# Keys of the second batch by TensorE, x1 of the last batch by VectorE, and a new order of steps

## The chip, the cores and the metric

The kernel runs on one core of a Trainium2 chip. The metric is the device time of one execution in microseconds (us). Its engines are TensorE (PE: matrix products), VectorE (DVE), ScalarE (ACT), GpSimd (POOL) and SyncE (SP, whose queue issues nearly all DMAs here, one after the other). On-chip memory is SBUF; products land in PSUM.

## The reference

Three blocks follow one another on 4 batches of 768 tokens with 384 channels, all in fp32:

```python
# 1. linear attention, 8 heads of 48 channels
state = alpha[:, :, t, :, None] * state + einsum('bhd,bhe->bhde', k_t, v_t)
y[:, :, t] = einsum('bhd,bhde->bhe', q_t, state)          # for t in 0..767
# 2. low-rank token mix (rank 32), then an MLP 384 -> 1536 -> 384
u = x + ((x.T @ U) @ V).T
x1 = u + maximum(u @ w_ch1, 0) @ w_ch2
# 3. phases and a complex token mix, then a channel product
theta = x1 @ w_theta
y = w_tok_r @ (x1 * cos(theta)) + w_tok_i @ (x1 * sin(theta))
u = x1 + y
out = u + maximum(u @ w_ch, 0)
```

## The kernel before, in words

**Layout.** Channels lie on the partitions. Each batch has three tiles of 128 channels, and so three stored head pairs (p0 to p2, two heads of 64 and 48 rows each); the rows that are left of three pairs make a fourth pair, p3, whose keys `kp` and queries `qp` are put together by small copies of 16 rows between tiles (line 241; its decays `tp`, line 306). Its result `xp` goes back into the three tiles `X` by six such copies (line 461).

**Attention.** Time is cut into 6 chunks of 128. Lines 227 and 230 load `al`, `kk`, `qq` and `vv`. Scans and products turn keys and queries into a form without the decay (`G`, line 265; `kk`, 267; `al`, 275; `qq`, 276). Per pair: scores A (line 326) and a mask into `Am` (332 to 336), keys turned by 128 x 128 (into `kt`), increments D (377), their scan into `S` (384 on ScalarE, 387 on VectorE), and Y (397 within a chunk, 405 from the state), copied into `X` or `xp` (407).

**Two ways to turn a tile.** TensorE multiplies it with the identity into PSUM and ScalarE copies it out (keys: 358 to 365; x1: 840). Or VectorE transposes blocks of 32 x 32 (`turn`, line 250), four small DMAs put them in place in DRAM (`place`, 257), and a load brings the turned tile back (keys: 344, then a copy of the spare part by ScalarE, 351; x1: 823). Batch 0's keys go the first way and those of batches 1 to 3 the second; x1 of batches 0 to 2 goes the second way and that of batch 3 the first.

**The rest.** `xt` (544) and `g` (551) are the rank-32 products and 527, 528 the lift that adds them. The MLP runs in halves of 384 tokens over 12 blocks: `h` and `acc`, each product as three in a 1-pass format with high and low parts (668 to 670). x1 is spilled to DRAM. Theta `th`, its sine and cosine (854 to 865), and the complex token mix as seven products `mx` (978), each with its own factor sums; some of these sums are made by accumulating DMAs on GpSimd's queue (908). Last the channel product `ch` and the result (1020).

**What sets the order.** Every part is a Python generator that issues some instructions at each step. `ORDER` is a string with one letter per step: D loads, P prepares, A and B are two pairs of attention in turn, R spare copies, U and L weights, 0, 1, 2 and K the rank products, M and N the two MLP halves, H theta, V and S factors and sums, G the seven products, Y and C the outputs. Where a generator needs something, it draws another one itself. Each engine and the SyncE queue take their instructions in the order in which the steps issue them. Tables such as `BY_Q` say for each operation whether VectorE (V) or GpSimd (P) does it; in `BY_A`, A stands for ScalarE and GpSimd. A DMA waits on one of eight semaphores in turn, so for the DMA eight before it.

Of the kernel before, what the change touches and what calls it, by code (L numbers as in the profile page):

```python
# [36 lines left out]


ORDER = """
DRAPRBURAARPPBARQDAAPBBBURBRARUBUPRAAPQUAUALABBUBBBAAQQAAABLBDABLPLLAPA01BDP01AL2200R11QL2LAL201AALPABR2B210BB  # L40
MLLLRRALLAMNLDLLAAMMQLRBPMMLBMMLBRLPNMMNQLLLLNLMNLLLNMMLLMLMNLMNLMMLMLMLMMTARAAAMPRMNBABBBBDTPBNANBATABQARWBNA
WBWPNNPKNKNABBNNNQNKNKBNKKKKKDBAKRRDAPRPRBAKNBBBBAAKAKAKAQBANMBMPBPMMAMMRBMDQAKMAMBRAPABAMRBWPAMMBMABRKWBKAQBW
MANMABFABBNKABXKAKAMKFFBTTNFMBTTMMKKBNKWNNKNMMNNKKKNKMTKNKMMMNWTWTKNNMKNMNKNMMNHMNNMMTNKKNNNNMMTTTHMKTTMMHKMKM
MMHKMKMNMMTNTNMKNKKTNNNKHMNNMKNNNHKNKNNNHNNKNHNKKNNNHTHNTMTNNMNHNHNMNXHHMMTHMTTTMHTNTMTNNTHNTMTTMHHTMNMHHMMHNM
VVNNNTHTHHMTTMHHXMTHMTTMNNVNNHNVMHXTNHHHVMVVMHMHNHGNVVHGHTGVGHGGHHTGGGHHVGGVHTHGGVVHHGGGSVVVHGHGGHSVGSVVGVVGVH
HGGHGVVHSHGHVXVGGXVGVGSSGGGVVGGGGGGGGVGGVVGVGVVVGGGSGVYVGSGVGGGSVGGSVVVVXGGGGGVVGGGGGVVGGVGVGGGVSVGGGGGGVVGGVS
VGVGVVGGVVVGGGGGGVGGGGGVYGVGGVTVVVVVGGTGGGGVGVVVYGTVVGGYVVGYVGGGGGVGGGTCCGYYVCGCCGYCCCYCCGCGGGGGGYCCCCCYCYCCCC
CCCC
"""
# [7 lines left out]
BY_X = "PPPPVVVPVVVVPPPVVVVPVVVV"
BY_T = "PVPVPVVVVPVPPVVPVVVVPVVVVVVVVVVVVPVVVVVVVP"
BY_U = "VVVVVPPVVPPV"
BY_S = "VVPVPPVPVPVVVPPPVPVPPPVV"  # L60
# [9 lines left out]
def linear_attention_moe_kernel(ctx, tc, aT, kT, qT, aF, kF, qF, vP, vT, U, V4, w1, w2, wth, wtr, wti, wch, out):  # L70
# [208 lines left out]
    def prep_k(b, i):  # L279
        pr[b, i] = ld.pop((b, i)) + (T("G"),)  # L280
        if b + i:
            scale_k(b, i, 0, S)
        else:
            pool.memset(pr[b, i][3][:, HT - 1:HT], 1.0)
            for x, y in halves(b, i):
                scale_k(b, i, x, y)
                scale_q(b, i, x, y)
        KK[b, i] = pr[b, i][1]
        if b:
            t, keysT[b, i] = turn(KK[b, i][:, 0:(NC - 1) * C], f"kt{b}_{i}", 128)  # L290
# [26 lines left out]
    def att_pe(b, p):  # L317
# [105 lines left out]
        yield
        ms.append(scores(1))
# [273 lines left out]
    def contract(pend=pend):  # L698
        b, hf, f, h = pend.pop(0)
        if f == 0:  # L700
            acc[b, hf] = [PS("acc") for _ in range(KD)]
        for j in range(KD):
            w = [x[:, j * 128:(j + 1) * 128] for x in W2[f]]
            three(acc[b, hf][j][:, 0:HT], w, (h[:, 0], h[:, 1]), f == 0, f == NF - 1)
        done_with(h)
        used(W2, f)
        if f == NF - 1:
            for j, t in enumerate(acc.pop((b, hf))):
                x = X[b][j][:, hf * HT:(hf + 1) * HT]
# [106 lines left out]
    def theta(b):  # L816
        for hf in range(2):
            xs = []
            turned_x = b in range(B - 1)
            for s in range(hf * 3, hf * 3 + 3) if turned_x else ():  # L820
                if b % 2 == 0:
                    ZR[b // 2, s] = two(T("zr"))
                sync.dma_start(ZR[b // 2, s][:, b % 2], turned[f"x1t{b}_{hf}"][(s - hf * 3) * C:(s - hf * 3 + 1) * C])
            for j in range(KD):
                t = two(T("x1s", F32R))
                split(X[b][j][:, hf * HT:(hf + 1) * HT], t[:, 0], t[:, 1],
                      e_lo=dve if b in range(B) and BY_X[(b * 2 + hf) * KD + j] == "V" else pool)
                xs.append(t)
            yield 600
            for q in range(3):  # L830
                s = hf * 3 + q
                th = PS("th")
                for j in range(KD):
                    w = TH[j]
                    l = xs[j][:, :, q * C:(q + 1) * C]
                    three(th[:, 0:DM], (l[:, 0], l[:, 1]), (w[:, 0], w[:, 1]), j == 0, j == KD - 1)
                if not turned_x:
                    xt = PS("x1t")
                    for j in range(KD):
# [24 lines left out]
                for t, x in ((zi, zi), (zr, co)):  # L864
                    dve.tensor_tensor(out=t, in0=x, in1=xc, op=ALU.mult)
                done_with(n)
                if not turned_x:
                    done_with(xt)
                if b in range(B):
                    made.add((b, s))  # L870
                    if b == B - 1:
                        plus(ZR[1, s], ZI[1, s])
                else:
                    zh, zl = two(T("zh", F32R)), two(T("zl", F32R))
                    split(z, zh, zl, e_hi=act)
# [130 lines left out]
    def outputs():  # L1006
        for k, hf in ((0, 0), (1, 1), (1, 0), (0, 1)):
            while len(CH) < KD:
                next(gens["T"], None)
            while (k, hf, KD - 1) not in UQ:  # L1010
                next(gens["Y"], None)
            us = [UQ.pop((k, hf, j)) for j in range(KD)]
            for q in range(2):
                for e in range(KD):
                    t = PS("ch")
                    for j in range(KD):
                        w = CH[j][:, :, e * 128:(e + 1) * 128]
                        three(t[:, 0:HT], (w[:, 0], w[:, 1]), (us[j][0][:, q], us[j][1][:, q]), j == 0, j == KD - 1)
                    ot = T("ot")[:, 0:HT]
                    dve.scalar_tensor_tensor(out=ot, in0=t[:, 0:HT], scalar=0.0, in1=XQ[k, hf][e][:, q],  # L1020
                                             op0=ALU.max, op1=ALU.add)
                    done_with(t)
                    sync.dma_start(out[2 * k + q, e][:, hf * HT:(hf + 1) * HT], ot)
                    done_with(ot)
                    yield
# [379 lines left out]
```

## Time and profile before

| | |
|---|---|
| median of 3 runs | 667.82 us (667.09 to 669.35) |
| profiled execution | 665.01 us |
| its span | 662.9 us |
| TensorE busy | 630.8 us, 95% of the span |
| VectorE, ScalarE, GpSimd busy | 438.0, 267.2, 156.1 us |
| TensorE's mean granted clock | 0.987 |

The profile is of one execution; 2.1 us of it lie outside the span. TensorE is the busiest engine by far, so what counts is the time in which it waits, and the stretches in which its granted clock is below 1. Busy time of the other engines counts only where TensorE waits for them.

### The profile page before, as it was taken

To read this page: it belongs to the slowest core of one execution; us is meant where nothing else is said; L and a number is where in the kernel's file an instruction comes from. 1 tells how busy PE (TensorE), PEld (TensorE's weight loads), DVE (VectorE), ACT (ScalarE), POOL (GpSimd) and SP (SyncE) were. 2 spreads that over 40 slices of the span, in tenths; PEclk is the share of its full clock that TensorE was granted. 3 is DMA by queue.
4 is the path that set the end of the run, shared out by engine and by line. 5 is a ranking of instruction groups with operands and counts; after the bars stand their busy time and mean duration, and the time that the engine had idled before them with its cause. 6 is when DMAs were issued, how large, how long until landed. Compare 5 with 4: busy or idle time off the path is not lost.

```text
span 662.9 us, 11739 instructions
## 1 busy us (share of the span) xinstructions
PE 630.8 (95%) x4485; PEld 607.0 (92%) x4485; DVE 438.0 (66%) x727; ACT 267.2 (40%) x552; POOL 156.1 (24%) x181
## 2 busy tenths in 40 slices
PE   2887999999998999999999999999999999999996
PEld 1776899989897899999999999999999989999996
DVE  7869799766775643825545658574878677895433
ACT  2555644243543442221513334445577343573010
POOL 4413323212412030010000001112235544443020
PEclk9968999999998999999999999999999999999999
DMA  8678486467855654343413166554326925200222
GB/s 307 238 219 256 143 268 191 115 169 165 265 148 167 121 175 108 53 115 83 144 47 73 20 208 211 134 165 145 108 60 124 264 55 120 48 1 0 108 79 106
DMA packets 124032, 91.55 MB, mean 138 GB/s; under 512 B 86272, under 2 KB 104576, under 8 KB 123968
## 3 DMA queue, kind: packets, MB, share of 16 engines
q1 hardware_dynamic: 120512, 82.46, 41.6%
q0 software_dynamic: 3456, 8.26, 6.9%
q8 instruction: 37, 0.61, 0.4%
q14 instruction: 27, 0.22, 0.1%
HBM read 59.42 MB, written 19.46 MB: 119 GB/s over the span
## 4 chain that ended last, share of the span: by engine, by line
PE 85%; DMA 6%; DVE 3%; issue 2%; POOL 2%; ACT 1%; SPq 1%; POOLq 0%; ACTq 0%; DVEq 0%
PE mx L978 13%; PE h L668 8%; PE acc L668 8%; PE acc L670 8%; PE acc L669 8%; PE h L670 8%; PE h L669 8%; PE A L326 4%; PE Y L397 3%; PE Y L405 3%; PE ch L670 2%; PE ch L668 2%; PE ch L669 2%; DMA zr<-zi 2%; PE D L377 2%
## 5 line engine op out<-in xcount | busy, mean ns | idle before, releaser
L978 PE MATMUL mx<-wp,zh 128*128 128x384 f32 x504 | 128.5, 336 | 1.7 <-ACT wp L176 1.4
L690 DVE SCALAR_TENSOR_TENSOR hh<-h,hh 128x384 fp32r<-128x384 f32 x96 | 52.3, 551 | 82.5 <-ACT hh L689 80.7
L668 PE MATMUL h<-uh,wh 128*128 128x384 f32 x288 | 98.0, 340 | 0.0
L668 PE MATMUL acc<-hh,wh 128*128 128x384 f32 x288 | 97.8, 340 | 0.0
L669 PE MATMUL acc<-hh,wh 128*128 128x384 f32 x288 | 96.9, 336 | 0.0
L670 PE MATMUL acc<-hh,wl 128*128 128x384 f32 x288 | 96.9, 336 | 0.0
L669 PE MATMUL h<-uh,wh 128*128 128x384 f32 x288 | 96.4, 335 | 0.0
L670 PE MATMUL h<-uh,wl 128*128 128x384 f32 x288 | 96.4, 335 | 0.0
L689 ACT ACTIVATE hh<-h 128x384 fp32r<-128x384 f32 x96 | 46.4, 490 | 114.4 <-PE h L670 110.6
L978 PEld LDWEIGHTS mx<-wp,zh 128*128 128x128 f32 x504 | 90.4, 188 | 2.3 <-issue 2.2
L978 PE MATMUL mx<-wp,zl 128*128 128x384 f32 x252 | 84.2, 334 | 0.0
L668 PEld LDWEIGHTS acc<-hh,wh 128*128 128x128 f32 x288 | 54.3, 189 | 1.6 <-issue 0.3
L668 PEld LDWEIGHTS h<-uh,wh 128*128 128x128 f32 x288 | 54.0, 188 | 1.8 <-issue 0.3
L670 PEld LDWEIGHTS acc<-hh,wl 128*128 128x128 f32 x288 | 54.5, 189 | 0.0
L669 PEld LDWEIGHTS acc<-hh,wh 128*128 128x128 f32 x288 | 54.4, 189 | 0.0
L669 PEld LDWEIGHTS h<-uh,wh 128*128 128x128 f32 x288 | 54.1, 188 | 0.0
L670 PEld LDWEIGHTS h<-uh,wl 128*128 128x128 f32 x288 | 54.1, 188 | 0.0
L978 PEld LDWEIGHTS mx<-wp,zl 128*128 128x128 f32 x252 | 47.3, 188 | 0.0
L333 POOL TENSOR_SCALAR_AFFINE_SELECT Am<-Am 128x384 f32<-128x384 f32 x40 | 25.5, 665 | 77.5 <-ACT Am L332 77.4
L177 POOL TENSOR_TENSOR x1s<-Y,x1s 128x384 fp32r<-128x384 f32 x8 | 8.0, 1025 | 151.3 <-ACT x1s L176 121.8
L177 DVE TENSOR_TENSOR wp<-cv,wp 128x384 fp32r<-128x384 f32 x32 | 24.9, 782 | 12.1 <-ACT wp L176 12.1
L1020 DVE SCALAR_TENSOR_TENSOR raw<-ch,xq 128x384 f32<-128x384 f32 x24 | 13.4, 557 | 28.1 <-PE ch L670 27.9
(187 smaller groups left out, 1209.9 us busy)
## 6 DMA issues: line engine op xcount, KB each, us to landing
raw<-in_w SPq DMA_DIRECT2D x12, 768.0 KB, 4.7
vv<-in_vP SPq DMA_DIRECT2D x16, 291.0 KB, 6.5
raw<-in_wti SPq DMA_DIRECT2D x12, 384.0 KB, 3.5
raw<-in_wtr SPq DMA_DIRECT2D x12, 384.0 KB, 3.7
xq<-x1d SPq DMA_DIRECT2D x24, 192.0 KB, 5.0
out<-raw SPq DMA_DIRECT2D x24, 192.0 KB, 1.8
al<-in_aT SPq DMA_DIRECT2D x11, 384.0 KB, 4.9
kk<-in_kT SPq DMA_DIRECT2D x11, 384.0 KB, 5.4
```

The costliest lines, as they stand in the source:

```text
L177: (e_lo or dve).tensor_tensor(out=lo, in0=src, in1=hi.bitcast(F32), op=ALU.subtract)
L326: pe.matmul(ts[h][:, j * C:(j + 1) * C], k[r, c], q[r, c], start=True, stop=True)
L333: pool.affine_select(out=m, in_=m, pattern=[[0, 3], [1, C]], compare_op=ALU.is_ge, fill=0.0, base=0, channel_multiplier=-1)
L397: pe.matmul(t[64 * h:64 * h + n, o], v[:, c * 96 + h * D:c * 96 + h * D + n], ms[g][h][:, j], start=(j == 0), stop=(c == 0), skip_group_ch ...
L405: pe.matmul(t[64 * h:64 * h + D, o], st[64 * h:64 * h + D, :, c - 1], q[64 * h:64 * h + D, c * C:(c + 1) * C], start=False, stop=True, ski ...
L668: pe.matmul(out, a[0], b[0], start=first, stop=False)
L669: pe.matmul(out, a[0], b[1], start=False, stop=False)
L670: pe.matmul(out, a[1], b[0], start=False, stop=last)
L689: act.activation(h[:, 0], t[:, 0:HT], ACTF.Relu)
L690: dve.scalar_tensor_tensor(out=h[:, 1], in0=t[:, 0:HT], scalar=0.0, in1=h[:, 0].bitcast(F32), op0=ALU.max, op1=ALU.subtract)
L978: pe.matmul(t[:, 0:HT], x[:, q, c], w[:, y], start=f, stop=l, skip_group_check=True)
L1020: dve.scalar_tensor_tensor(out=ot, in0=t[:, 0:HT], scalar=0.0, in1=XQ[k, hf][e][:, q], op0=ALU.max, op1=ALU.add)
```

## The change

It has four parts. The keys of batch 1 are turned by TensorE, as those of batch 0. x1 of batch 3 is turned by VectorE and DMAs, as that of the others. In the last group of outputs, the two tiles of 384 columns of the last channel block become one of 512 and one of 256. And nearly all of `ORDER` and of the tables is new; of these a line or two stands here.

```diff
 ORDER = """
-DRAPRBURAARPPBARQDAAPBBBURBRARUBUPRAAPQUAUALABBUBBBAAQQAAABLBDABLPLLAPA01BDP01AL2200R11QL2LAL201AALPABR2B210BB
+PAQRURPRBADAUUPQRRADARBRPABBPAARDABARBUUPQUBBUABBABBABQPBLAAAALLBAA00B1DP1ARL0L2P0R2BBARLB11R22QLDLAL201LLALP0
 ...
-BY_K = "PVPVVVVVPVVV"
+BY_K = "VVVVVPVVVVVV"
-BY_Q = "VVPVVPPVPPPV"
+BY_Q = "VPPVVPPPPPPV"
 ...
@@ prep_k
-        if b:
+        if b > 1:
             t, keysT[b, i] = turn(KK[b, i][:, 0:(NC - 1) * C], f"kt{b}_{i}", 128)
             place(t, keysT[b, i], 0)
@@ attention of a pair
-            if b + p and not b:
+            if b + p and b < 2:
                 across(1)
 ...
-        if p < KD and (b or p == 0):
+        if p < KD and (b > 1 or b + p == 0):
             across(1)
@@ contract
-                if b in range(B - 1):
+                if b in range(B):
                     place(*turn(x, f"x1t{b}_{hf}", DM), j * 128)
@@ theta
-            turned_x = b in range(B - 1)
+            turned_x = b in range(B)
@@ outputs
-            for q in range(2):
-                for e in range(KD):
+            parts = [(e, q * HT, (q + 1) * HT) for q in range(2) for e in range(KD)]
+            if (k, hf) == (0, 1):
+                parts = [p for p in parts if p[0] < KD - 1] + [(KD - 1, 0, 512), (KD - 1, 512, 768)]
+            for e, x, y in parts:
 ...
```

Three places show how instructions move. A row is line, instruction, what it writes and reads, shape, count; a number at a name is that of the buffer.

The first is SyncE's queue from the first copy of `tp` on, before and then now. `al`, `kk`, `qq`, `vv` are attention loads, here those of batch 1's first tile; `kp`, `qp` and `tp` are the copies for p3 of batch 0.

```order
L306 DMA tp3_93<-tp0_90 16x5 x2
L227 DMA al_192<-in_aT 128x768
L227 DMA kk_193<-in_kT 128x768
L227 DMA qq_194<-in_qT 128x768
L230 DMA vv_198<-in_vP 128x582
L241 DMA kp_200<-kk_114 16x384 x2
L241 DMA qp_213<-qq_115 16x384 x2
L241 DMA kp_200<-kk_114 16x384 x2
L241 DMA qp_213<-qq_115 16x384 x2
L306 DMA tp3_93<-tp1_91 16x5 x2
```

```order
L306 DMA tp3_93<-tp0_90 16x5 x2
L241 DMA kp_204<-kk_114 16x384 x2
L241 DMA qp_209<-qq_115 16x384 x2
L306 DMA tp3_93<-tp1_91 16x5 x2
L241 DMA kp_204<-kk_114 16x384 x2
L227 DMA al_247<-in_aT 128x768
L227 DMA kk_248<-in_kT 128x768
L227 DMA qq_249<-in_qT 128x768
L230 DMA vv_253<-in_vP 128x582
L241 DMA qp_209<-qq_115 16x384 x2
```

The four loads have moved behind the first copies of `tp`, `kp` and `qp`.

The second is TensorE around the first `xt`, before and then now. X_309 and X_321 are the first channel tile of batch 0, `kT` is a key transpose, A the scores, D the increments of batch 1.

```order
L377 MATMUL D<-vv,kt 64x48
L377 MATMUL D<-vv,kt 48x48
L544 MATMUL xt<-ident,X_309 128x128 x3
L544 MATMUL xt<-ident,X_358 128x128 x3
L544 MATMUL xt<-ident,X_309 128x128 x3
L544 MATMUL xt<-ident,X_358 128x128 x3
L544 MATMUL xt<-ident,X_524 128x128 x6
L551 MATMUL g<-xs,uf 128x128 x18
```

```order
L405 MATMUL Y<-qq,S 48x128 x10
L358 MATMUL kT<-ident,kk 128x128 x5
L326 MATMUL A<-qq,kk 128x128 x12
L544 MATMUL xt<-ident,X_321 128x128 x6
L358 MATMUL kT<-ident,kk 128x128 x5
L544 MATMUL xt<-ident,X_417 128x128 x6
L377 MATMUL D<-vv,kt 64x48
```

Key transposes of batch 1 and its first scores stand ahead of and between the `xt` of the first two tiles; before, the `xt` of all three stood together behind D.

The third is ScalarE at two places where a turned key tile (`kt`, by line 351) is copied. Before, the second tile of batch 3 (kt_2313 is what the load brought), ahead of the state `S` of batch 3's first pair:

```order
L332 COPY Am1_82<-A_2340 128x384
L332 COPY Am1_82<-A_2341 128x384
L176 CAST uh_2353<-X0_758 128x384
L689 ACTIVATE hh_2388<-h1_2378 128x384
L351 COPY kt_1998<-kt_2313 128x10x16
L384 COPY S_2404<-tp12_102 128x288
```

Now, the third tile of batch 2 (kt_1864) and the state of its second pair:

```order
L332 COPY Am3_84<-A_1828 128x384
L332 COPY Am3_84<-A_1829 128x384
L689 ACTIVATE hh_1861<-h1_1851 128x384
L311 ACTIVATE al_1577,sq_89<-al_1577 128x768
L312 ACTIVATE G_1692,sq_89<-G_1692 128x767
L351 COPY kt_1083<-kt_1864 128x5x32
L384 COPY S_1891<-tp9_99 128x288
L176 CAST xs_1897<-xt_1867 128x384
```

The copy of `S_2404` stood right behind a key copy. In the new order the state of batch 3's first pair (now `S_2307`) is copied ten rows ahead of the second tile's key copy, and at the earlier place shown, `S_1891` stands right behind one.

## Rows read from the trace of the kernel before

**Rows 1.** TensorE's waits: engine, line, what it waited for: us in total, times, longest.

```profile
PE kT L358 <- DVE kk L267: 6.6, 1, 6.6
PE A L326 <- DMA qp<-qq: 5.6, 2, 5.2
...
PE xt L544 <- DMA X<-xp: 4.3, 1, 4.3
PE Y L405 <- DVE S L387: 2.3, 1, 2.3
PE mx L978 <- ACT wp L176: 1.4, 1, 1.4
```

**Rows 2.** Windows: stretch, length, busy time (instructions) by engine, TensorE's clock, DMA share, GB/s.

```profile
36.12:44.40 8.28, 7.94 (x74) 7.11 (x76) 3.70 (x8) 5.47 (x12) 2.79 (x3) 0.50 0.61 154
54.69:58.00 3.31, 3.31 (x16) 3.31 (x17) 3.24 (x5) 1.91 (x5) 0.55 (x1) 0.50 0.78 125
58.00:73.00 15.00, 15.00 (x146) 11.94 (x144) 12.53 (x21) 9.82 (x25) 4.74 (x4) 1.00 0.89 283
73.00:100.00 27.00, 27.00 (x214) 25.45 (x211) 23.92 (x36) 13.22 (x29) 8.18 (x8) 1.00 0.64 197
210.24:215.00 4.76, 4.76 (x38) 4.17 (x40) 4.28 (x4) 0.96 (x2) 2.04 (x2) 0.65 0.69 254
```

**Rows 3.** The chain of waits, 28 to 74 us: start us, us, what.

```profile
28.73 6.27 DMA vv<-in_vP
35.02 2.06 DMA qp<-qq
37.22 2.90 PE A L326 x22
...
49.23 5.32 DMA X<-xp
...
70.83 0.65 PE h L527 x2
...
73.17 0.38 PE h L668
```

**Rows 4.** Timeline of SyncE's queue at 15 and 186 us: start, us, DMAs issued.

```profile
14.93 0.34 SPq L227 DMA_DIRECT2D al<-in_aT  x1
...
186.44 7.26 SPq L257 DMA_DIRECT2D x1t<-tx  x12
```

**Rows 5.** Timeline of TensorE at 28 and 509 us: start, us, line, operation, count.

```profile
27.87 0.77 PE L358 MATMUL kT<-ident,kk 128*128 128x128 f32 x5
28.57 1.61 PE L326 MATMUL A<-qq,kk 48*128 48x128 f32 x24
...
508.88 0.52 PE L840 MATMUL x1t<-ident,X 128*128 128x128 f32 x3
509.15 0.60 PE L978 MATMUL mx<-wp,zh 128*128 128x384 f32 x2
```

**Rows 6.** Timelines of VectorE at 15 us and GpSimd at 24 us.

```profile
15.33 0.96 DVE L276 TENSOR_TENSOR qq<-qq,al 128x768 f32<-128x768 f32 x1
...
23.73 1.82 POOL L276 TENSOR_TENSOR qq<-qq,al 128x768 f32<-128x768 f32 x1 [2.17 <-DVE tp L303]
```

**Rows 7.** The chain of waits, 204 to 209 us.

```profile
204.71 4.00 DMA kt<-kt
208.74 0.32 ACT kt L351
```

**Rows 8.** DMA issues of the page: line, engine, count, KB each, us to landing.

```profile
zr<-x1t SPq DMA_DIRECT2D x12, 192.0 KB, 3.9
zr<-zi POOLq DMA_DIRECT2D x6, 384.0 KB, 4.6
```

**Rows 9.** The chain of waits, at 517 us and its end.

```profile
516.57 10.27 DMA zr<-zi
...
657.15 0.56 DVE raw L1020
```

More of the change, by code (lines that the diff above doesn't have):

```diff
@@ L39 @@
 ORDER = """
-DRAPRBURAARPPBARQDAAPBBBURBRARUBUPRAAPQUAUALABBUBBBAAQQAAABLBDABLPLLAPA01BDP01AL2200R11QL2LAL201AALPABR2B210BB
[L41 to L44, printed above, removed]
@@ L45 @@
-VVNNNTHTHHMTTMHHXMTHMTTMNNVNNHNVMHXTNHHHVMVVMHMHNHGNVVHGHTGVGHGGHHTGGGHHVGGVHTHGGVVHHGGGSVVVHGHGGHSVGSVVGVVGVH
-HGGHGVVHSHGHVXVGGXVGVGSSGGGVVGGGGGGGGVGGVVGVGVVVGGGSGVYVGSGVGGGSVGGSVVVVXGGGGGVVGGGGGVVGGVGVGGGVSVGGGGGGVVGGVS
-VGVGVVGGVVVGGGGGGVGGGGGVYGVGGVTVVVVVGGTGGGGVGVVVYGTVVGGYVVGYVGGGGGVGGGTCCGYYVCGCCGYCCCYCCGCGGGGGGYCCCCCYCYCCCC
-CCCC
-"""
-BY_K = "PVPVVVVVPVVV"
-BY_Q = "VVPVVPPVPPPV"
-BY_W = "VPPPPVVPVPPP"
-BY_A = "AAVVVVVAAAAVAVAVAAVVAAAAAAVAAVAA"
-BY_Z = "PVVVPVPPVVPPVVVVVVVVVVVVVPVVVVVPVPVVPVVVVV"
@@ L57 @@
[L57 to L60, printed above, removed]
+PAQRURPRBADAUUPQRRADARBRPABBPAARDABARBUUPQUBBUABBABBABQPBLAAAALLBAA00B1DP1ARL0L2P0R2BBARLB11R22QLDLAL201LLALP0
+1MA2MBMALRLLANMQALLALMNNMPLLLAMBLMBPMMBBMLLRQNLLLNLNMNNLMLMLLLNMLMLMMLLNMLRMTMMMBPMBABBAATDPNNQRNARBTNBAABPNWA
+WWNNARNBAAPBBANAKKQANBKANKABKAKKAKRDKPBKRNKPARKBNBAAKDBKBNBAPBAQMMBBPMBAAMKRRMDAKAQBMBMPMXPBAMBAQFRBMMKMMWBNAA
+MMBNFARBNFAABWBWMBBATTMAKMBMKTFNKNBNWTWNKKMTNTNKTNKNKNTHKKKWMMTNMMKNKNNKNNTMNKKKKNMNKKKNMKNKNMNMMNTMMKKNTMHNNH
@@ new lines @@
+MMTTNKNNKMKNMNNHNHTNNKMTHTMNMNMTMMMMMKMMKNNKNHNMKTNHKMNNNHHHHMMHMNMTNMHMTNXMTTTTNNTMHNNTNHTMHMNHTTMHMVHHNXMHTN
+MNNTHTHNHTTNNHHHNTMMHVVNMTHHMMVHMTTNTHNVNVMHMNNHHGHVNGGVHGVHVTHVHHGGGGGHGXVVGHTHVHGGHGVHGGHGSGVSGVGGHVGSVVVGHV
+GGHGVVHVGGHHHSVSGVGXGGGGGGVXSVGGVGGVVGGGVGGGVXGVSGVVVGGGVVVGGGSVVGGGGGVVVGGGSGVGVVVVGGVGGGGGGSSVGGVVVVGGVGVGSG
+GVVGVGGVVGVGGGGGVGGGGVGVGVYGVVGGVGGGGVVTVGGTGVGGGVGGGYGTVGVVYTGGVCCCGGYVCCGGVYGGYCYCCVYCYCGGGGGGYYCCCYCCCCCCCC
+CCCC
+"""
+BY_K = "VVVVVPVVVVVV"
+BY_Q = "VPPVVPPPPPPV"
@@ L61 @@
+BY_W = "VPPPPPVPPPPV"
+BY_A = "VVAVAAVVAAVAAVVAAAAAVAAAVAAVVAVA"
+BY_Z = "PVVVPVPVVPVVPVVVVVPVVVVVVPVVVVVPPPVVVVPVPP"
+BY_X = "PVVPVPPPVVPPVPVPPPVVVVVV"
+BY_T = "VVVPVPPPVVPPPPVVVVPVPVVVPVVVVVVPPVVVVVVVPV"
+BY_U = "PPVVPVVVVVPP"
+BY_S = "VVVPPPVVVVPPVVPPPPVPPVVV"
 MAGIC = 12582912.0
@@ L1011, in outputs @@
                 next(gens["Y"], None)
-            us = [UQ.pop((k, hf, j)) for j in range(KD)]
-            for q in range(2):
-                for e in range(KD):
[L1015 to L1025, printed above, removed]
+            us = [[x.rearrange("p a b -> p (a b)") for x in UQ.pop((k, hf, j))] for j in range(KD)]
+            parts = [(e, q * HT, (q + 1) * HT) for q in range(2) for e in range(KD)]
+            if (k, hf) == (0, 1):
+                parts = [p for p in parts if p[0] < KD - 1] + [(KD - 1, 0, 512), (KD - 1, 512, 768)]
+            for e, x, y in parts:
+                t = PS("ch")[:, 0:y - x]
+                for j in range(KD):
+                    w = CH[j][:, :, e * 128:(e + 1) * 128]
+                    three(t, (w[:, 0], w[:, 1]), (us[j][0][:, x:y], us[j][1][:, x:y]), j == 0, j == KD - 1)
+                ot = T("ot")[:, 0:y - x]
+                dve.scalar_tensor_tensor(out=ot, in0=t, scalar=0.0,
+                                         in1=XQ[k, hf][e].rearrange("p a b -> p (a b)")[:, x:y],
+                                         op0=ALU.max, op1=ALU.add)
+                done_with(t)
+                for q in range(x // HT, (y - 1) // HT + 1):
+                    a, z = max(x, q * HT), min(y, (q + 1) * HT)
+                    sync.dma_start(out[2 * k + q, e][:, hf * HT + a - q * HT:hf * HT + z - q * HT], ot[:, a - x:z - x])
+                done_with(ot)
+                yield
             done_with(*[t for u in us for t in u], *XQ.pop((k, hf)))
```

## The prediction

> **What bounds the kernel now.** I read the table of waits first. TensorE is the bound: it sits idle in few places, and each has a name. Behind the wait for the first keys (6.6), which the change leaves, stand one wait of 5.2 us (5.6 in all) for the last `qp` copy, one of 4.3 for the last copy into `X`, one of 2.3 for the scan of `S` and one of 1.4 for a `wp` factor [rows 1]. Next the windows, for the clock: after each of the first three waits TensorE's granted clock is at its lower level (0.50, which is 1.2 of 2.4 GHz), for 8.28, 3.31 and part of 4.76 us, while elsewhere it is 1.00; after the 1.4 there is no such stretch [rows 2]. A stretch costs its busy time times the missing clock: 7.94 × 0.50 = 3.97, 3.31 × 0.50 = 1.66, 4.76 × 0.35 = 1.67. So the three waits are worth 5.6 + 4.3 + 2.3 = 12.2 us of idleness and 7.3 of slow clock, 19.5 together, and that is all that an order can win there. Third the chain of waits from 28 to 73 us, which says why the first two exist: SyncE's queue stands on `vv`, issued at 28.73 and landed 6.27 later, before the last `qp` copy can go; then the copies into `X` land 5.3 after their issue, behind loads [rows 3].
>
> **The change part by part, on the profiled execution (665.01 us; 2.81 under the median of the runs, 667.82).**
>
> *The start.* The first block of four loads for the second batch, issued from 14.93 [rows 4], now stands behind five groups of spare copies, so by the queue's spacing it goes out near 21. The second block waits for the first one's landings and is issued at 25 to 28, about as in the kernel before (27.1 to 28.7); its `vv` at 5 us (an estimate between 3.9, the landing of a smaller load [rows 8], and the 6.27) lands near 33, and with two copies behind it `qp` is there near 35.0 (34.0 to 37.2) instead of 37.1. From the scores to the first MLP product the kernel before takes 73.17 − 37.22 = 35.95 [rows 3]; less 3.97, 4.3 and 1.66 this is 26.0 of work. The order lists what the new one does there: the ten products of `D_463`, 0.4 us, come into it, ten more key transposes too, and two products of the lift (0.65 [rows 3]) drop out behind. Five transposes take 28.57 − 27.87 = 0.70 from start to start [rows 5], so ten are 1.4. That is 27.1. The wait for `X` should be gone: the fourth pair is now finished ahead of the third, its copies go out near 43 instead of 48.7, and a batch of transposes and scores stands between.
>
> Two costs stay. VectorE now makes both halves of the first keys ahead of the second keys (two products of half a tile, 0.96 together by the whole one: +1.0 at 12.9 us), and GpSimd scales one more `qq` at 1.82 instead of 0.96 [rows 6], and TensorE waits for one of them. Both lie ahead of the scores on `qp` and so are covered by the wait for it: TensorE was ready for them 5.6 us before 37.22, at 31.7, and is now ready near 33. From 33 to 35.0 it is still idle for 2 us: a wait of 2.3 brought the slow clock, one of 1.4 did not [rows 1, 2], so I take half of that stretch's price, 2.0. VectorE is busy 12.5 of 15 us, then 23.9 of 27 [rows 2], and must now deliver masks, `xs` and weights faster, with only two key transposes less by then: 1.5 of new waits (0 to 2.5). First MLP product: 35.0 + 27.1 + 2.0 + 1.5 = 65.6, so **−7.6** (−11.1 with neither; −2.4 at 37.2 + 27.1 + 4.0 + 2.5).
>
> *The wait at 208.* ScalarE's queue holds the copy of a turned key tile ahead of a copy of `S`; the tile's load, issued at 204.71, lands 4.00 later, and the copy at 208.74 frees everything [rows 7]. The load was late because SyncE's queue had issued twelve x1 pieces for 7.26 us ahead of it, and more [rows 4]. The new order puts that copy of `S` ten rows ahead of the key copy: **−3.95** (2.28 and 1.67). But the same pairing now stands earlier, at `kt_1864`, directly ahead of `S_1891`, and in SyncE's queue six X copies, four key pieces and twelve x0 pieces of some 0.6 each stand ahead of that load. I put it 2 to 3 us late: **+2.5**, between 0 and 5.7 (a wait of 4.0 with a slow stretch).
>
> *Last batch's x1.* Six VectorE transposes, 24 small DMAs and six loads come, 18 TensorE transposes go. The latter take (509.15 − 508.88) / 3 = 0.09 each [rows 5], 1.6 in all. VectorE is not the bound there, and the pieces are issued when SyncE is mostly free: nothing, unless a load is late, and one takes 3.9 to land [rows 8]. With the five key transposes that are left (0.7) and the lift's 0.65 this makes −1.6 + 0.7 + 0.65, some **−0.2**. All 15 transposes added against all 18 removed are 2.1 − 1.6 = +0.5 by these rows. The Trainium skill, VectorE: DVE Perf Modes, section "The three transpose paths", puts a TensorE transpose of 128 by 128 at 390 ns (bf16). By that, an estimate, the 18 would be 7.0 and the 15 would be 5.9, −1.2 instead of +0.5, and the sum 1.7 lower; the trace has 0.14 and 0.09 from start to start, where they follow one another, and decides.
>
> *The end chain.* By the order the last theta stands 3.1 us of TensorE work nearer to the first product that needs it. The wait of 1.4 [rows 1] can vanish, being short, or grow by that and bring a slow stretch, 3.1 + 1.7. I take **+1.5** (−1.4 to +4.8), half of the 3.1.
>
> *The last outputs.* The last VectorE instruction takes 0.56 for 384 columns [rows 9]; 256 make 0.37 in proportion, and the last DMA is smaller: **−0.2** (0 to −0.5).
>
> Sum: −7.6 − 3.95 + 2.5 − 0.2 + 1.5 − 0.2 = −7.95, so 657.1 for the profiled execution and **659.9** on the median's scale.
>
> **The rivals.**
>
> *The start hardly moves.* `vv` lands as late as before and the slow stretch stays whole: −2.4 instead of −7.6, 665.1. For it: the same eight loads stand ahead of the last `qp`. Against: the copies that now stand ahead of the loads were behind them.
>
> *The copies into X stay behind the weights.* Two 768 KB weight loads stand directly ahead of them in the new queue too. If the drain sets the landing and not the issue, X comes near 51 instead of 47, the wait of 4.0 and its 1.7 of slow clock stay: 659.9 + 5.7 = 665.6. For it: 5.32 for 48 KB [rows 3]. Against: the attention loads that stood between are issued earlier. The Trainium skill, DMA: Bandwidth & Descriptors, section "Queues, rings and completion order", says descriptors of one queue are consumed in ring order; by that rule this case is the one to expect whenever the queue is full, and the trace's 5.32 agrees with it.
>
> *Supply gives it back.* TensorE starts its products 7.6 us earlier, VectorE, busy 89% of the time there, does not, and the weights and masks make TensorE wait until the lead is gone: only the 3.95 − 2.5 and small terms stay, 667.5. For it: 23.92 of 27 [rows 2]. Against: of TensorE's waits none but that of 2.3 and those of the first 13 us is for VectorE for longer than 0.3 [rows 1].
>
> *Slower.* The accumulations of the last batch's z on GpSimd's queue stand at the end of the chain. One of them took 10.27 where such a transfer's median is 4.6 [rows 8, 9], 5.7 longer, while the loads of `xq` ran. If the last batch's six loads come into the same stretch and two accumulations in a row are late by as much, that is 11.4 of waiting and two slow stretches of 1.7, 14.8 in place of 1.5: −7.95 + 13.3 = +5.4, 673.2. It decides from 8 us of added wait on. For it: the last theta stands nearer to its use. Against: 24 pieces of 48 KB are little, and the wait there is 1.4 now.
>
> **How the numbers follow.** The forecast has 0.55, the start that hardly moves 0.15, X behind the weights 0.08, supply 0.10, slower 0.12. The bounds of the forecast's own terms give about 655 to 665; to leave out no more than 2 in 10, the range goes from 651 (nothing new waits: −11.1 − 3.95 − 1.4 − 0.7 = −17.2) to 668.5, which takes in the first three rivals. A measurement tells 0.3%, 2.0 us, from no change. Faster: 0.55, 0.12 of 0.15, 0.05 of 0.08 and nothing of the rest, 0.72. Same: 0.03, 0.03 and 0.06 of supply, 0.12. Slower: 0.12 and 0.04 of supply, 0.16.
>
> **What would show it.** In the profile after: the `qp` wait under 2.5 us and the landing at 34 to 36; no wait of `xt` for X over 1 us; the first MLP product at 63 to 67; no wait for `S` near 200; a wait of `Y` for `S` near 155 with a stretch at 0.50 behind it, or none; the `wp` wait between 0 and 4.5. It is wrong if the first MLP product comes after 70, or if TensorE has new waits over 5 us between 65 and 200 or behind 480.

## The result and the profile after

The changed kernel is slower: 672.31 us (median of 10 runs, 670.65 to 675.14) against 668.4 for the kernel before, beside it on the same chip (10 runs, 666.48 to 673.11). The ratio is 1.0052, with a 95% interval from 1.0027 to 1.0077. I had forecast 659.9.

The profiled execution of the changed kernel is the longest of the ten, 675.14 us. A second one took 671.35 and shows the same waits, so below it stands beside the first wherever a time rests on one execution.

TensorE's waits in the changed kernel, in the columns of [rows 1]:

```profile
PE kT L358 <- DVE kk L267: 7.6, 1, 7.6
...
PE D L377 <- DMA kt<-kt: 2.0, 1, 2.0
PE A L326 <- issue: 1.7, 1, 1.7
PE D L377 <- DVE S L387: 1.6, 1, 1.6
...
PE A L326 <- DMA qp<-qq: 1.5, 1, 1.5
PE h L533 <- DVE hh L690: 1.4, 1, 1.4
PE A L326 <- ACT X L530: 1.1, 1, 1.1
PE Y L397 <- DVE D L385: 0.9, 1, 0.9
...
PE mx L978 <- DVE wp L177: 0.7, 1, 0.7
...
PE xt L544 <- DMA X<-xp: 0.5, 1, 0.5
```

The big waits of [rows 1] are gone: `qp` 5.6 has become 1.5 (3.2 with the one called "issue" ahead of it), `X` 4.3 is 0.5, and the wait for `S` at 208 us does not occur. In their place stand many small ones, none of which looks like a cause. The windows after three of them, as [rows 2]:

```profile
38.07:44.90 6.83, 6.83 (x85) 6.61 (x84) 3.75 (x9) 3.29 (x9) 2.81 (x3) 0.50 0.96 300
...
79.03:82.45 3.42, 3.42 (x13) 3.42 (x12) 3.27 (x7) 2.12 (x7) 0.00 (x0) 0.50 0.00 0
...
154.13:157.54 3.41, 3.41 (x19) 3.32 (x15) 1.44 (x2) 0.87 (x3) 0.99 (x2) 0.50 0.33 70
```

Again three stretches at the lower level of the clock, 13.7 us with half of it lost, 6.8; before it was 7.3. So neither the waits of that table nor the clock tell where some ten microseconds went. TensorE's busy time has grown, from 630.8 to 637.3 us, although the work, as measured below, differs by only 0.6: part of what is lost counts as busy.

I therefore measured each kernel against its own work. Every TensorE instruction gets the median distance from its start to the next start, over all instructions of its line in the traces compared here; their running sum is the work, and it is subtracted from the real time. What is left is the time lost so far, in us, after 50, 100, ... us of work:

| kernel (profiled execution) | 50 | 100 | 250 | 480 | 610 |
|---|---|---|---|---|---|
| before | 25.1 | 24.6 | 22.3 | 23.5 | 26.1 |
| changed, first execution | 20.1 | 23.3 | 30.3 | 32.5 | 36.1 |
| changed, second execution | 17.6 | 20.9 | 26.1 | 28.2 | 32.3 |

(A median is not a minimum, so a column may fall.) The changed kernel is 5.0 to 7.5 ahead after 50 us of work, gives 3.7 to 3.8 back by 100, loses 7.5 to 9.3 against the kernel before between 100 and 250, and 2.0 to 2.4 over the rest. The stretch that decides is that between 100 and 250, real time 120 to 275. There the chain of waits to look at is SyncE's queue. Its timeline, in the columns of [rows 4], before:

```profile
129.79 2.05 SPq L257 DMA_DIRECT2D kt<-tx  x4
...
133.16 6.20 SPq L257 DMA_DIRECT2D x1t<-tx  x12
...
144.50 2.72 SPq L461 DMA_DIRECT2D X<-xp  x4
...
148.58 0.53 SPq L344 DMA_DIRECT2D kt<-kt  x1
...
150.50 7.91 SPq L257 DMA_DIRECT2D x0t<-tx  x12
```

and in the changed kernel:

```profile
122.65 4.27 SPq L189 DMA_DIRECT2D raw<-in_wth  x3
134.83 2.04 SPq L257 DMA_DIRECT2D kt<-tx  x4
136.97 7.07 SPq L257 DMA_DIRECT2D x1t<-tx  x12
...
149.31 0.49 SPq L344 DMA_DIRECT2D kt<-kt  x1
150.22 1.22 SPq L241 DMA_DIRECT2D raw<-qq  x2
152.19 3.72 SPq L461 DMA_DIRECT2D X<-xp  x6
156.01 1.26 SPq L344 DMA_DIRECT2D kt<-kt  x1
157.36 2.59 SPq L257 DMA_DIRECT2D kt<-tx  x4
160.08 7.36 SPq L257 DMA_DIRECT2D x0t<-tx  x12
```

TensorE enters this stretch ahead of the kernel before, but the queue is 4 to 10 us behind with the x1 pieces, X and x0. The load of the key tile is only 0.7 later, but the first product `D` behind it is due earlier: it starts at 153.64, as soon as the tile is there, and in the kernel before at 157.09 without a wait. The queue stands still from 126.9 to 134.8, until VectorE has turned the tile for `kt`:

```profile
133.96 0.84 DVE L250 STREAM_TRANSPOSE tx<-kk 128x640 f32<-128x640 f32 x1
```

In the kernel before VectorE did this at 128.91, 5 us earlier. So some of the lateness comes into the queue from VectorE; no run moves that alone. Then the queue issues almost without a pause until 175 us, 0.6 us for each small DMA. Key tiles, X, x0 and the buffers that these copies give back all hang on it. ScalarE shows two of those who wait, the last column being the idle time and what ended it:

```profile
153.53 0.33 ACT L351 COPY kt<-kt 128x160 f32<-128x160 f32 x1 [3.42 <-DMA kt<-kt]
...
162.16 0.49 ACT L689 ACTIVATE hh<-h 128x384 fp32r<-128x384 f32 x1 [7.16 <-DMA kt<-tx]
```

The second is the MLP's `hh`: it gets a buffer that a turned tile `tx` had held, and must wait until SyncE's queue has placed that tile.

### The profile page after: what moved, and what is told of

Its sections match the earlier page's. It is cut to its first block, busy times and chain, and to the rows that moved or that the text cites. A ratio compares the mean times of both kernels' runs of the same rounds, so it can differ in the third digit from the quotient of the medians.

```text
span 673.4 us, 11755 instructions
## 1 busy us (share of the span) xinstructions
PE 637.3 (95%) x4482; PEld 608.2 (90%) x4482; DVE 448.2 (67%) x723; ACT 268.2 (40%) x559; POOL 174.1 (26%) x188
## 4 chain that ended last, share of the span: by engine, by line
PE 54%; DVE 6%; DMA 3%; issue 2%; ACT 2%; POOL 2%; SPq 1%; DVEq 0%; POOLq 0%; ACTq 0%
PE mx L978 10%; PE acc L668 5%; PE acc L669 5%; PE h L668 5%; PE acc L670 5%; PE h L669 5%; PE h L670 5%; PE ch L670 2%; PE ch L669 2%; PE ch L668 2%; PE th L670 1%; PE th L669 1%; PE th L668 1%; DMA zr<-zr 1%; DVE zl L177 1%
## 5 line engine op out<-in xcount | busy, mean ns | idle before, releaser
L177 POOL TENSOR_TENSOR x1s<-Y,x1s 128x384 fp32r<-128x384 f32 x11 | 12.4, 1146 | 142.2 <-ACT x1s L176 124.1
L333 POOL TENSOR_SCALAR_AFFINE_SELECT Am<-Am 128x384 f32<-128x384 f32 x38 | 22.9, 628 | 97.3 <-ACT Am L332 97.2
L587 DVE SCALAR_TENSOR_TENSOR cv<-raw,cv 128x384 int32<-128x384 int32 (+2 forms) x41 | 30.9, 780 | 0.1
L1022 DVE SCALAR_TENSOR_TENSOR raw<-ch,xq 128x384 f32<-128x384 f32 (+2 forms) x22 | 12.3, 558 | 26.1 <-PE ch L670 25.6
```

Of the source, the lines that this page charges most:

```text
L177: (e_lo or dve).tensor_tensor(out=lo, in0=src, in1=hi.bitcast(F32), op=ALU.subtract)
L333: pool.affine_select(out=m, in_=m, pattern=[[0, 3], [1, C]], compare_op=ALU.is_ge, fill=0.0, base=0, channel_multiplier=-1)
L587: dve.scalar_tensor_tensor(out=t, in0=lo, scalar=29, in1=t, op0=ALU.logical_shift_right, op1=ALU.bitwise_or)
L1022: dve.scalar_tensor_tensor(out=ot, in0=t, scalar=0.0, in1=XQ[k, hf][e].rearrange("p a b -> p (a b)")[:, x:y], op0=ALU.max, op1=ALU.add)
```

## The experiments

Ratios are to the kernel before, run beside each on the same chip, with 95% intervals. Orders and tables are left out of the diffs.

**The changed kernel once more.**

> The changed kernel once more, for a second trace. If its stalls belong to its order, the same places show waits again: the first MLP product at 68 to 70 us, a wait of TensorE for a turned key tile at 152 to 156 with a stretch at 0.50 behind it, and over 4 us of idleness of TensorE between 150 and 235. If the first trace was an unlucky execution (it was the longest of ten, 675.1 against 672.3), the waits between 150 and 235 shrink to under 2 us and the execution comes near 671 or less.

671.35, with the waits of the first execution: 2.29 for the key tile at 151.5, 1.13 at 74.2, slow stretches behind both. The waits belong to the kernel. The first MLP product came at 66.69, earlier than expected. Of the 3.8 us between the two, 2.5 were lost in the first 50 us of work and 1.8 between 100 and 250; 0.5 came back behind 480.

**Code and order apart.** `edits_old_order` is the changed code with the order and tables of before, `new_order_only` the reverse.

> The three edits of the code with the order and the tables of before. Theory (the new order is what costs): no slower than before, ratio 0.992 to 1.001, since 12 small copies and three loads leave the crowded first 60 us. Rival (the edits cost: ScalarE copies of the added transposes, x1 of the last batch coming late): ratio 1.003 to 1.010, with new waits of TensorE for kt or zr.

> The order and the tables of the changed kernel with the code of before. Theory (the order costs): slower than before by 0.5 to 2%, since the order was also written without the key copies of batch 1 in SyncE's queue. Rival (the edits cost): within 0.3% of before or faster.

1.0173 [1.0145, 1.0201] and 1.0249 [1.0210, 1.0287]. New waits of TensorE, first with the old order, then with the new order alone:

```profile
PE th L668 <- ACT x1s L176: 4.4, 4, 1.6
PE mx L978 <- ACT wp L176: 4.0, 1, 4.0
```

```profile
PE xt L544 <- DMA X<-xp: 9.5, 1, 9.5
PE Y L397 <- DVE D L385: 3.8, 1, 3.8
```

Each half alone is worse than both together: with the old order x1 by VectorE makes theta and the factors late, and without the new keys the new order waits 9.5 for X. Neither part can be blamed alone.

**The parts on their own.** `b_keys` is the kernel before with the key edit alone, `b_x1` with the x1 edit alone; `a_no_x1` is the changed kernel without the x1 edit.

```diff
-        if b:                                   # b_keys
+        if b > 1:
-            if b + p and not b:
+            if b + p and b < 2:
-                if b in range(B - 1):           # b_x1 (a_no_x1: the reverse)
+                if b in range(B):
-            turned_x = b in range(B - 1)
+            turned_x = b in range(B)
```

> The kernel before with the keys of batch 1 turned by TensorE and nothing else (old order, old tables). The run with all three edits in the old order was 5.8 us ahead of before at the first MLP products, and lost that and 14 us more behind 470 us, at theta and the factors. Theory (the key edit is the gain, x1 of the last batch the loss in this order): ratio 0.988 to 0.995, no new waits behind 460 us. Rival (the key edit brings something of the late loss): 0.998 or more.

> The kernel before with x1 of the last batch turned by VectorE and DMAs and nothing else. Theory: TensorE's order in the end was written for the other way, so theta waits for x1s and the factors come late: ratio 1.015 to 1.03, waits of th for ACT x1s over 3 us and of mx for wp over 3 us. Rival (the loss needs the key edit too): within 0.5% of before.

> The changed kernel with x1 of the last batch turned by TensorE as before, all else as changed. Theory (the new order was written with this edit, and nothing of its loss against before comes from it): no faster than the changed kernel, 1.004 to 1.02 of before, with waits of mx behind 480 us where the changed kernel has 0.9 at most. Rival (the edit costs in the new order as it does in the old one): 0.985 to 0.998.

0.9990 [0.9966, 1.0014], 1.0185 [1.0148, 1.0222] and 1.0099 [1.0062, 1.0136]. With the old order the key edit loses 2.7 us less in the first 100 us of work (21.9, before 24.6), but its work is 2.5 us longer: the first MLP product starts at 72.99, before at 73.11, and nothing is gained. The x1 edit costs 1.9% with the old order and nothing visible with the new: without it the changed kernel is no faster.

**A waiter freed, and the next.** `a_kt_early` puts one letter of the order seven places ahead, so that the key tile at 153 us is loaded before a block of attention loads. `a_hh_slot` keeps `hh` off buffers last held by `tx`. `a_both` has both.

```diff
-...BPMBABBAATDPNNQRNARBTN...                   # a_kt_early
+...BPMBABBAATADPNNQRNRBTN...
-            i = free[kind].pop(0)              # a_hh_slot
+            k = 0
+            if kind == "s" and name == "hh":
+                k = next((m for m, v in enumerate(free["s"]) if last.get(v) != "tx"), 0)
+            i = free[kind].pop(k)
```

> The changed kernel with one letter of the order moved seven places forward: the load of the first turned key tile of batch 2 stands ahead of five attention loads and four small copies in SyncE's queue instead of behind them, and is issued some 5 us earlier; TensorE's own order is the same. Theory (the wait of 2.3 us for that tile at 152 us and the slow stretch behind it are SyncE's order): that wait is gone and no stretch at 0.50 stands at 152 to 156; 4 us less than the changed kernel, ratio to before 0.997 to 1.001. Rival (what is saved is waited for again at the next state or load): the wait goes, the time stays, 1.003 to 1.007.

> The changed kernel with one rule in the choice of buffers: a tile hh of the MLP does not take the buffer that a turned tile (tx) gave up last, if another is free. Theory (in the new order hh takes the buffer of a turned tile, whose small copies still stand in SyncE's queue, so ScalarE waits 6.6 us for them at 159 us and 4.6 at 200): these two waits of ScalarE go; the wait for the key tile at 152 stays; 2 to 5 us less than the changed kernel, ratio to before 0.998 to 1.002. Rival (TensorE is held up there by the key tile alone): no change, 1.004 to 1.007.

> The same rule, and the load of the first turned key tile of batch 2 seven steps earlier. Theory: the two waits stood one behind the other, so that either alone gave way to the other; together 6 to 10 us less than the changed kernel, ratio to before 0.990 to 0.997, no stretch at 0.50 between 100 and 230 us. Rival (a third thing, SyncE's queue itself, takes their place): 1.000 or more, with new waits of TensorE of over 4 us in all between 150 and 180.

1.0074 [1.0050, 1.0098], 1.0078 [1.0049, 1.0106] and 1.0096 [1.0059, 1.0133]: no gain. In `a_kt_early` the wait for the key tile is gone and another has grown; TensorE's wait, then ScalarE's between 100 and 250 us:

```profile
PE Y L397 <- DVE D L385: 5.2, 1, 5.2
```

```profile
ACT hh L689 <- DMA kt<-tx: 10.7, 1, 10.7
```

In `a_hh_slot` the wait for the key tile has grown to 2.8. In `a_both` neither is left, and TensorE waits for the next ones:

```profile
PE D L383 <- DVE S L393: 2.8, 1, 2.8
PE acc L674 <- ACT hh L695: 1.9, 1, 1.9
PE Y L403 <- DVE D L391: 1.7, 1, 1.7
```

A wait that moves on whenever its waiter is freed points to what all of them hang on.

**Past the queue, and the start.** `a_x1_gpsimd_queue` issues the pieces of batch 0's x1 and batch 1's x0 on GpSimd's queue. `a_load_late` moves a letter D twelve places back, so that all copies for `qp` stand ahead of the second block of loads; `a_three` adds that to `a_both`.

```diff
-            sync.dma_start(d[:, o + r:o + r + 32]...      # a_x1_gpsimd_queue
+            (q or sync).dma_start(d[:, o + r:o + r + 32]...
-PAQRURPRBADAUUPQRRADARBRPABBPAARDABARB...                # a_load_late
+PAQRURPRBADAUUPQRRAARBRPABBPAARDDABARB...
```

> The changed kernel with the 36 small copies of x1 of batch 0 and x0 of batch 1 issued from GpSimd's queue instead of SyncE's (some 0.6 us each, 22 us of SyncE's queue between 137 and 204). Theory (SyncE's queue is late there and holds up key tiles and loads): the waits of TensorE between 150 and 235 fall from 9 us to under 3 and the ratio to before becomes 0.990 to 0.999. Rival (VectorE's own order holds up TensorE there): the waits stay, ratio 1.003 to 1.008. Second rival (GpSimd's issuing holds up its products): new waits behind POOL.

> The changed kernel with one letter D moved 12 places back: the second block of attention loads of batch 1 stands behind the last copy of qp in SyncE's queue instead of ahead of it. Theory (the last qp copy is held by the load eight DMAs before it, whatever the order of the first block): it lands at 31 to 34 us instead of 36 to 38, the 1.5 us wait for it goes and with it the stretch at 0.50 at 36 to 43; 3 to 6 us less at the first MLP product, ratio to before 0.995 to 1.001. Rival (the moved loads are late for the scores of batch 1 and the wait turns up there): the first MLP product as early as in the changed kernel, 1.003 to 1.007.

> All three: the rule for buffers, the early key tile, the late block of loads. If the three are separate, 9 to 15 us less than the changed kernel, ratio to before 0.983 to 0.993. If supply (VectorE, weights) takes what the start wins, no less than with the first two.

1.0150 [1.0112, 1.0188], 1.0107 [1.0068, 1.0146] and 1.0113 [1.0074, 1.0151]. The first settles nothing: the loads left in SyncE's queue now waited for buffers that the pieces on the other queue gave back late. In `a_load_late` the wait for `qp` is gone, but the loads that had been ahead of it are late, issued from 31.45 and not from 27.18. A `vv` right behind them takes 9.4 to land, the copies into X go out after it, and TensorE waits for them (the first MLP product comes at 70.82):

```profile
PE xt L544 <- DMA X<-xp: 4.5, 1, 4.5
```

The first 50 us are a choice of who waits for the same queue, too.

**The queue made shorter.** x1 is needed late (by theta, from 270 us), so its pieces can be put in place late. In `a_x1_whole` batch 0's first x1 tiles go to DRAM as VectorE left them, in 3 DMAs instead of 12, and the 3 loads at theta become 12 that put the blocks in place. `b_x1_whole` is the kernel before with the same edit, `b_keys_x1_whole` adds it to `b_keys`, `a_both_x1_whole` to `a_both`.

```diff
+    def whole(b, hf):
+        return (b, hf) == (0, 0)
 ...
-                    place(*turn(x, f"x1t{b}_{hf}", DM), j * 128)
+                    t, d = turn(x, f"x1t{b}_{hf}", DM)
+                    if whole(b, hf):
+                        sync.dma_start(d[j * 128:(j + 1) * 128], t)
+                        done_with(t)
+                    else:
+                        place(t, d, j * 128)
 ...
+                if whole(b, hf):
+                    for r in range(0, C, 32):
+                        x = (s - hf * 3) * C + r
+                        sync.dma_start(ZR[b // 2, s][r:r + 32, b % 2].rearrange("p (i q) -> p i q", q=32),
+                                       d[:, x:x + 32].rearrange("(i p) q -> p i q", p=32))
```

> The changed kernel, but the first batch's first x1 tiles (twelve pieces of 0.6 us in SyncE's queue from about 134 us) are written to DRAM as VectorE left them, in 3 DMAs, and put in place by the 12 loads at theta (from about 270 us), when that queue is mostly free. So the queue is 9 DMAs, about 5.5 us, shorter at 135 to 142 us, and nothing else changes there. Theory (SyncE's queue is what TensorE loses to from 130 to 230 us): key-tile load, X copies, x0 pieces and the al loads go out 4 to 6 us earlier, the wait for the key tile near 152 (2.0 to 2.3) and the one for S near 174 (1.1 to 1.6) vanish with their slow clock, about 666 to 668, ratio 0.995 to 1.0. Rival (VectorE's and ScalarE's supply is the limit): the queue is earlier, but TensorE waits as long, for D, S or hh, within 1.5 us of the changed kernel, 671 to 673, ratio 1.004 to 1.007.

> The same edit on the version with the key-tile load one attention load earlier and hh kept off slots last held by a turned tile. Theory: each of these two only moved the wait to the next waiter of SyncE's queue; with the queue 5.5 us shorter none is late, and the time is 1 to 2 us under that of the edit alone, 664 to 667. Rival (supply): no better than that version without the edit, 672.5, ratio 1.006 to 1.01.

> The kernel before with the same edit. What the edit is worth without the change: the twelve pieces at 133 us there delay no product by more than a fraction, and the wait at 208 hangs on twelve other pieces (186 us). Theory: the same within 0.3 percent, or up to 2 us faster if the 208 wait shrinks because the queue in between is earlier, ratio 0.997 to 1.0. Rival (supply): exactly the same, 0.999 to 1.001. Slower (1.003 or more) if the twelve loads of 32 rows come late at theta.

> The kernel before with the key part of the change alone (0.999 without this edit) and the same edit. Theory: the key part's lead of 3 us at the start is given back by 300 us through SyncE's queue too; with the queue shorter 1 to 3 us of it stay, ratio 0.994 to 0.998. Rival: as without the edit, 0.998 to 1.001.

| | us | ratio | 50 | 100 | 250 | 480 | 610 |
|---|---|---|---|---|---|---|---|
| `a_x1_whole` | 666.11 | 0.9973 [0.9944, 1.0001] | 17.3 | 22.0 | 21.9 | 23.2 | 26.5 |
| `a_both_x1_whole` | 666.96 | 0.9988 [0.9964, 1.0012] | 17.7 | 20.9 | 23.0 | 25.2 | 29.1 |
| `b_x1_whole` | 665.54 | 0.9944 [0.9916, 0.9971] | 24.6 | 24.1 | 22.2 | 23.6 | 28.2 |
| `b_keys_x1_whole` | 663.38 | 0.9929 [0.9898, 0.9961] | 21.0 | 22.0 | 16.9 | 17.6 | 21.4 |

The five last columns are those of the table above, from one execution of each. Between 100 and 250 us of work the changed kernel lost 5.2 to 7.0 and loses nothing now. SyncE's queue in `a_x1_whole`:

```profile
135.69 1.48 SPq L718 DMA_DIRECT2D x1t<-tx  x3
...
143.10 0.38 SPq L347 DMA_DIRECT2D kt<-kt  x1
...
145.85 3.67 SPq L464 DMA_DIRECT2D X<-xp  x6
...
153.15 8.16 SPq L260 DMA_DIRECT2D x0t<-tx  x12
```

The key tile is loaded at 143.10 instead of 149.31, x0 starts at 153.15 instead of 160.08. TensorE's waits there, between 100 and 480 us:

```profile
PE h L536 <- DVE hh L693: 1.2, 1, 1.2
...
PE Y L400 <- ACT Am L335: 0.5, 1, 0.5
...
PE D L380 <- DVE S L390: 0.4, 1, 0.4
```

The wait for the key tile and its slow stretch do not occur, and freeing two waiters adds nothing any more. VectorE still turns the tile for `kt` late, at 132.67, and `hh` still waits 5.7 for a buffer: neither costs TensorE much once the queue behind them is shorter. `b_keys_x1_whole` is faster than the kernel before by 4.4 us at the median, and 2.2 shorter than `b_x1_whole` beside it: the key edit, worth nothing in `b_keys`, gains something here, though the two intervals overlap.

**Its issue or its bytes?** The edit also turns pieces of 128 bytes into rows of 1.5 KB. `a_x1_three_small` writes 3 DMAs in pieces of 128 bytes, `a_x1_twelve_rows` 12 DMAs of long rows; both are shown against `a_x1_whole`, the first without the loads that fit it.

```diff
-                        sync.dma_start(d[j * 128:(j + 1) * 128], t)
+                        for r in range(0, 128, 32):                         # a_x1_twelve_rows
+                            sync.dma_start(d[j * 128 + r:j * 128 + r + 32], t[r:r + 32])
+                        v = d.rearrange("(g m) w -> g (m w)", m=32)
+                        sync.dma_start(v[:, j * 4096:(j + 1) * 4096].rearrange("g (p q) -> p g q", q=32),
+                                       t.rearrange("p (g q) -> p g q", q=32))   # a_x1_three_small
```

> The changed kernel, the first batch's first x1 tiles written in 3 DMAs as in a_x1_whole, but in pieces of 128 bytes as in the changed kernel. Few DMAs in the queue, as much work of the DMA engines as before. Theory (SyncE's queue, 0.6 us for each DMA): as fast as a_x1_whole, 665 to 667.5, ratio 0.995 to 1.0, no wait for a key tile near 152. Rival (the DMA engines' work on small pieces): as the changed kernel, 671 to 673, ratio 1.004 to 1.007.

> The changed kernel, the same tiles written as rows of 1.5 KB as in a_x1_whole, but in 12 DMAs of 32 rows. As many DMAs in the queue as in the changed kernel, little work of the DMA engines. Theory (SyncE's queue): as the changed kernel, 670 to 673, ratio 1.003 to 1.007, with the wait for the key tile near 152 of about 2. Rival (the DMA engines' work): as fast as a_x1_whole, 665 to 667.5, ratio 0.995 to 1.0.

1.0009 [0.9982, 1.0036] and 1.0064 [1.0036, 1.0093]; between 100 and 250 us of work they lose 2.3 and 7.2. Three DMAs of small pieces take little more of the queue than three of long rows, 2.05 against 1.48. Twelve DMAs of long rows take nearly as long as twelve of small pieces, and the waits are back. The queue in either, then TensorE with the twelve:

```profile
134.44 2.05 SPq L719 DMA_DIRECT2D x1t<-tx  x3
```

```profile
134.57 6.64 SPq L719 DMA_DIRECT2D x1t<-tx  x12
```

```profile
PE Y L400 <- DVE D L388: 2.9, 1, 2.9
PE D L380 <- DMA kt<-kt: 1.7, 1, 1.7
```

So the number of DMAs decides in this stretch. The size of the pieces may add a little: `a_x1_three_small` lies 0.36% above `a_x1_whole`, with intervals that overlap. The Trainium skill, DMA: Bandwidth & Descriptors, section "Specifications", wants transfers of 512 bytes or more for the full rate. By that the long rows should have helped, and here they did not: twelve of them stay at 1.0064, against 1.0052 for the changed kernel.

## Why the prediction was wrong

*The start (−7.6).* The first MLP product began at 69.10 in the first execution and 66.69 in the second, against 73.17 [rows 3] and a forecast of 65.6, so 4.1 and 6.5 of the 7.6 came:

```profile
69.10 0.34 PE L668 MATMUL h<-uh,wh 128*128 128x384 f32 x1
```

The step "`qp` is there near 35.0" failed in the first execution, and came within its range (34.0 to 37.2) in the second. SyncE issued, in the first:

```profile
28.76 0.43 SPq L230 DMA_DIRECT2D vv<-in_vP  x1
...
34.99 1.21 SPq L241 DMA_DIRECT2D qp<-qq  x2
...
47.07 2.41 SPq L461 DMA_DIRECT2D X<-xp  x4
```

`vv` at 28.76 and `qp` at 34.99 are where [rows 3] has them (28.73, 35.02), as the rival "the start hardly moves" said. What held the copy is the load eight DMAs ahead of it, here `qq`, issued at 28.29: SyncE waited 2.0 for it, until 6.7 after its issue, where I had put 5 for `vv`. In the second execution `qp` was issued at 33.26. TensorE started on `qp` at 37.87 and 36.07 in the two executions, against 37.22. (The term "ready at 31.7" was read wrongly, too: the wait of 5.2 ended at 36.12, so TensorE had been ready at 30.9.) But the work from there to the first MLP product took 31.2 and 30.6, where I had 27.1 + 2.0 + 1.5 = 30.6 and the kernel before took 35.95. The wait for X went as forecast, 0.5 and none in the two executions, but in part by luck: its copies went out at 47.07 (45.20 in the second), not near 43, and in the first X was there at 51.9, where the rival that puts X behind the weights had it (near 51). TensorE came to it late itself, at 51.5. That rival's wait of 4.0 is out, its landing is not.

*Supply.* I had put 1.5 into the start for it. It came behind the first MLP product: the waits at 76.60 and 77.49 (1.14 and 0.44) and the 3.42 at half clock, 3.3 together. VectorE's queue had the scan of `al` ahead of `uh`, and so the `h` and `hh` behind it were late:

```profile
72.17 1.76 DVE L275 TENSOR_TENSOR_SCAN al<-al,ends 128x768 f32<-128x768 f32 x1
...
73.91 0.55 DVE L177 TENSOR_TENSOR uh<-h,uh 128x384 fp32r<-128x384 f32 x1
```

Of the lead of 5.0 and 7.5 after 50 us of work, 1.3 and 3.7 were left after 100. So the rival "supply" took back half of the lead or more, but at two waits and not by weights and masks.

*The wait at 208 (−3.95 + 2.5).* This is the step that failed by most. The old wait is gone as forecast. The one at `kt_1864` came, but smaller: that tile's load was issued at 169.99, and ScalarE shows the key copy and the copy of `S` behind it:

```profile
174.40 0.32 ACT L351 COPY kt<-kt 128x160 f32<-128x160 f32 x1 [3.22 <-DMA kt<-kt]
174.63 0.42 ACT L384 COPY S<-tp 128x288 f32<-128x288 f32 x1
```

TensorE waits 1.63 for that `S` (`D`, at 175.90; 1.09 in the second execution), and the clock stays at 1.00. The longest wait of the stretch, 1.98 at 153.64 and half of the 3.41 behind it, 3.7 together, is for another key tile, the first of batch 2, and no term of the sum stood for it. I had priced one waiter of a late queue, and a single tile was not what the lateness held: it held the earlier key tile, `hh` through its buffer, X, x0 and the later key tiles. In place of −1.45 for this stretch, the changed kernel lost 7.5 to 9.3 against the one before, between 100 and 250 us of work. I had the rows for the right question: SyncE's queue takes 7.26 for twelve pieces [rows 4], and the order showed how much stood ahead of that load. What I did not ask was how long that queue runs without a pause, and who else is in it.

*Last batch's x1 and the outputs (−0.2 each).* Nothing of either shows as a cost in the changed kernel. By the medians of the table its work is 0.6 longer, near the +0.5 that [rows 5] gave for all 15 transposes added and all 18 removed. The last VectorE instruction is 0.42, not 0.56 [rows 9]:

```profile
667.66 0.42 DVE raw L1022
```

The outputs were not tried apart.

*The end chain (+1.5).* The wait of 1.4 for `wp` [rows 1] became 0.7 for `wp`, 0.6 for `zl` and 0.3 for `raw`, with no slow stretch. From 480 to 610 us of work the changed kernel loses 3.6 to 4.1, the kernel before 2.6: +1.0 to +1.5. The rival "slower" had the sign of the result, but not its place: no two accumulations were late there.

With the second execution the account by the table is −7.5 + 3.8 + 7.5 + 0.9 + 1.5 = +6.2; with the 0.6 of added work that is 6.8, and the spans, 669.6 and 662.9, differ by 6.7. The medians lie only 3.9 apart; the profiled execution of before, 665.01, is below all ten of its runs here.

My own falsifier, new waits of over 5 us between 65 and 200, came true: 1.6, 2.0, 0.9 and 1.6 alone make 6.1 (5.3 in the second execution).

The 4.7 that `a_x1_whole` loses between 50 and 100 us of work has an account in its trace: the same two waits, 1.14 and 0.44, and behind them a granted clock of 0.50 from 74.76 to 81.59, which is 6.83 us and not 3.42, half of it lost. That makes 5.0.

What stays open: why `b_x1_whole` gains 0.56% when its one trace shows none of it (it still waits 3.0 for `S` at 210). The interval of `b_x1_whole` says that the kernel before pays for those twelve pieces too, about 3.7 us, while the changed kernel gains 0.8% by the same edit (0.9973 against 1.0052). With the edit in both, the changed kernel is still 0.3% longer than the kernel before (0.9973 / 0.9944), where it was 0.5% longer without. So the traces show that those pieces cost the changed kernel its time between 100 and 250 us of work; by the whole times they make only about half of the difference between the two kernels, and with intervals of 0.3% to either side that share is rough. The rest of it is not shown.

## What to carry to other kernels

A queue that issues one DMA after the other is an engine. Add up its issue time over the stretch in which it has no pause, and list everything that hangs on it, buffers to be given back too; a wait for one of its transfers is only the first of several, and freeing that one moves the wait to the next. What helps is to take DMAs out of the full stretch, and to put the work where the queue is idle: pieces that are needed 130 us later don't have to be placed now. And a lead at the start is worth only what the next supplier behind it can keep.

## What the runs showed of the hardware

- Twelve DMAs on SyncE's queue took 7.07 us in pieces of 128 bytes and 6.64 in rows of 1.5 KB, three took 1.48 and 2.05: 0.5 to 0.7 for each of these, in small pieces or in rows.
- The granted clock fell to its lower level after an idle time of 1.98 us (at 153.64) and after two of 1.14 and 0.44 with a product between them (at 77); it stayed at 1.00 after one of 1.63 (at 175.90). The length of a wait alone did not tell. Behind the same two waits the lower level lasted 3.42 us in the changed kernel and 6.83 in `a_x1_whole`.
- Two executions of the same kernel can differ by 2.5 us in the first 50 us of work alone, against 3.9 between the medians of the two kernels.
